# Real and imaginary PSUM tiles apart in a frequency-domain convolution with an MLP behind it, with taps between matmul groups and roots moved to GpSimd

## The chip, the cores and the metric

The kernel runs on one core of one Trainium2 chip. The metric is the device time of one execution in microseconds (us). The kernel before takes 347.24 us (median of the runs beside the changed kernel; 347.0 in the three runs that came first). A run that is more than 1.5% above the fastest of its kernel is labelled slow and left out of the ratios. Engines are called PE (TensorE matmul), PEld (its weight loads), DVE (VectorE), ACT (ScalarE) and POOL (GpSimd).

## The reference, cut to what matters

```python
S, D, ks, Dff = 2048, 512, 4, 1376                 # bfloat16 inputs, batch 1
kv = short_causal_conv(k, shift_k) * v             # 4 taps along the sequence
y  = irfft(rfft(kv padded to 2S) * rfft(ssm_k padded to 2S))[:S] + kv * ssm_D
h  = q + layernorm(q) * y
out = h + relu(layernorm(h) @ w1) @ w2
```

The kernel computes the long convolution as a two-stage DFT by matmul for `ssm_k` and for `kv`, a complex product, and a two-stage inverse DFT.

## The kernel before

These are the parts that the change touches. This program counts PSUM, the memory that matmuls write to, in banks of 512 fp32 values for each partition, and its largest pools hold eight of them. `u` and `psy` below are two banks each, with two buffers, which fills all eight.

```python
# product stage, 16 rounds kp
def product(kp):
    u = psum.tile([P, 2, 2, 256], F32, tag="u")            # real half s=0, imaginary half s=1
    usb = prod.tile([P, 2, 256 - NJ, 2], F32, tag="usb", bufs=2)
    for s in range(2):
        stage2(u[:, s, :, :], a1x, kp, s)                   # 4 matmuls of 256 columns, PE
        uj = u[:, s, :, :].rearrange("p k j -> p j k")
        nc.scalar.copy(out=usb[:, s, :, :], in_=uj[:, po, :])     # ACT, for GpSimd
        # ... t[s] = u * kf: columns dv on DVE from PSUM, columns po on GpSimd from usb

def finish():                                              # two rounds later
    psy = psum.tile([P, 2, 512], F32, tag="psy")
    for s, (a, b, m) in enumerate(...):
        # two matmuls of 512 columns into psy[:, s, :]
        nc.scalar.copy(out=kf[:, s, :, 2*kp:2*kp+2], in_=psy[:, s, :]...)   # ACT
# ...
# stage 1 of a DFT: 8 groups of 64 small matmuls (32 rows, 64 columns), 4 evacuations each
# taps: 16 blocks of 4 matmuls of 512 columns and one DVE multiply, after stage 2 of k
# ...
def inv2(q):                                               # pz is ONE tile of four banks
    for l4 in range(4):
        # 64 matmuls (32x32 by 128 columns) into pz[..., l4, :]
        nc.scalar.copy(out=zt[:, 4*q + l4, :]..., in_=pz[:, :, l4, :]...)   # ACT

def rstd(mv, r, q):                                        # row norms' roots
    nc.scalar.activation(out=r[:, ts, :], in_=mv[:, ts, 1:2], func=ACT.Sqrt, ...)
    nc.vector.reciprocal(out=r[:, ts, :], in_=r[:, ts, :])
# MLP: PSUM tiles of one bank, three buffers; transposes of the norm one token tile at a time, one buffer
```

## Time and profile before

The profiled run has a span of 344.8 us. The stages, read from the timeline, each from its first matmul to the first of the next (inverse stage 2 up to its own last matmul, and the entry from there):

| stage | before, us | granted PE clock |
|---|---|---|
| up to the first product | 87.2 | 0.5 to 1.0 by stage |
| products, 16 rounds | 100.1 | 0.50 |
| inverse stage 1 | 18.3 | 0.89 |
| inverse stage 2 | 35.2 | 0.54 |
| entry to the MLP | 6.65 | |
| MLP | 97.3 | 0.97 |

The first line of the page's busy part says why the average misleads; each entry is an engine, its busy time, its share of the span, and its instructions:

```profile
PE 254.9 (74%) x3094; PEld 169.8 (49%) x3104; DVE 163.0 (47%) x313; ACT 135.0 (39%) x240; POOL 54.3 (16%) x75
```

PE is the busiest with 74%, but 67 of its busy 255 us lie in a product stage that runs at half clock, where the same matmuls take up to twice as long. A busy share doesn't say whether an engine is the bound or is only slow; the clock row, the waits and the rounds do.

### The profile page before, as it was taken

How to read it: one execution, taken by the hardware profiler on the slowest of the kernel's cores; microseconds unless marked ns; L12 is line 12 of the kernel's file. 1: busy time of each engine (PE TensorE's matmuls, PEld its weight loads, DVE VectorE, ACT ScalarE, POOL GpSimd, SP SyncE). 2: the span in 40 equal slices, each digit the busy share in tenths (PEclk: the TensorE clock that was granted, in tenths of full speed). 3: DMA queues.
4: the chain of work that ended last, by engine and by line, in shares of the span. 5: the costliest groups of instructions: out<-in, count | busy, mean ns of one | idle time of the engine just before them, and what ended most of it. 6: DMA issues, size and time to landing. Idle time of an engine off the chain costs nothing.

```text
span 344.8 us, 7155 instructions
## 1 busy us (share of the span) xinstructions
PE 254.9 (74%) x3094; PEld 169.8 (49%) x3104; DVE 163.0 (47%) x313; ACT 135.0 (39%) x240; POOL 54.3 (16%) x75
## 2 busy tenths in 40 slices
PE   0765999966566666667667986666597887897994
PEld 0754994555544444445444983444243443343441
DVE  8966577677443223332331984400753483582111
ACT  3964560256123322233224892222353073162420
POOL 4694000000343223332333000000000000000000
PEclk9955899985555555555555995555589999999999
DMA  8990008000000000000002980000001101101101
GB/s 254 205 163 4 3 0 127 0 3 6 2 0 0 1 0 0 0 0 2 0 0 59 199 316 4 4 4 4 0 0 28 34 0 33 30 0 32 31 15 46
DMA packets 23663, 13.88 MB, mean 40 GB/s; under 512 B 19056, under 2 KB 22480, under 8 KB 23504
## 3 DMA queue, kind: packets, MB, share of 16 engines
q1 hardware_dynamic: 22560, 13.36, 16.3%
q8 instruction: 24, 0.39, 0.5%
q10 hardware_dynamic: 1072, 0.07, 0.3%
q14 instruction: 7, 0.06, 0.1%
HBM read 7.08 MB, written 2.10 MB: 27 GB/s over the span
## 4 chain that ended last, share of the span: by engine, by line
PE 66%; ACT 10%; DVE 10%; issue 3%; ACTq 0%; DVEq 0%
PE ps2m L495 11%; PE ps1m L482 10%; PE psy L332 10%; PE pz L420 7%; PE u L232 6%; PE psi L393 5%; DVE t L322 5%; PE pkv L282 4%; PE u L234 4%; ACT kf L334 3%; ACT zt L423 3%; PE ps2k L232 3%; PE ps2k L234 2%; ACT hlnT L470 2%; DVE st L433 2%
## 5 line engine op out<-in xcount | busy, mean ns | idle before, releaser
L322 DVE TENSOR_TENSOR t<-u,kf 128x704 fp32r<-128x704 f32 x32 | 28.5, 892 | 64.2 <-ACT usb L318 64.1
L482 PE MATMUL ps1m<-hlnT,w 128*128 128x512 bf16 (+1 forms) x175 | 41.3, 396 | 4.3 <-ACT h1T L484 3.3
L495 PE MATMUL ps2m<-w,h1T 128*128 128x512 bf16 (+1 forms) x169 | 38.8, 379 | 0.4
L322 POOL TENSOR_TENSOR t<-usb,kf 128x320 fp32r<-128x320 f32 x32 | 28.3, 886 | 65.0 <-ACT usb L318 64.9
L332 PE MATMUL psy<-t,ipos 128*128 128x512 f32 x48 | 29.2, 684 | 10.9 <-ACT kf L334 10.9
L420 PE MATMUL pz<-bp,ecore 32*32 32x128 f32 x1024 | 24.3, 406 | 11.8 <-ACT zt L423 10.9
L484 ACT ACTIVATE h1T<-ps1m 128x512 bf16<-128x512 f32 (+1 forms) x44 | 25.8, 595 | 18.0 <-PE ps1m L482 17.7
L232 PE MATMUL u<-a1x,c2n 128*128 128x256 f32 x32 | 16.0, 499 | 21.7 <-DVE t L322 21.7
L482 PEld LDWEIGHTS <-w 128*128 128x128 bf16 (+1 forms) x176 | 18.2, 104 | 26.9 <-issue 8.4
L498 DVE TENSOR_TENSOR o<-ps2m,xh 128x512 bf16<-128x512 f32 x16 | 11.1, 692 | 41.6 <-PE ps2m L495 41.6
L334 ACT CAST kf<-psy 128x512 fp32r<-128x512 f32 x32 | 19.2, 601 | 29.3 <-PE psy L332 29.3
L495 PEld LDWEIGHTS <-h1T 128*128 128x128 bf16 (+1 forms) x176 | 17.0, 98 | 20.0
L318 ACT COPY usb<-u 128x160 f32<-128x160 f32 x32 | 9.3, 292 | 42.8 <-PE u L234 42.8
L420 PEld LDWEIGHTS pz<-bp,ecore 32*32 32x32 f32 x1024 | 15.0, 134 | 20.8 <-ACT zt L423 17.6
L332 PEld LDWEIGHTS psy<-t,ipos 128*128 128x128 f32 x48 | 13.3, 318 | 22.7 <-ACT kf L334 22.5
L232 PEld LDWEIGHTS u<-a1x,c2n 128*128 128x128 f32 x32 | 10.0, 311 | 26.4 <-DVE t L322 26.4
L433 DVE BATCH_NORM_STATS2 st<-xh 128x6 f32<-128x512 bf16 x32 | 19.7, 678 | 0.0
L423 ACT CAST zt<-pz 128x512 bf16<-128x512 f32 x16 | 9.4, 584 | 24.2 <-PE pz L420 24.2
L393 PE MATMUL psi<-dre,kf 128*128 128x256 f32 x64 | 17.1, 304 | 0.7 <-ACT kf L334 0.7
L429 DVE RECIPROCAL rstd<-rstd 128x4 f32<-128x4 f32 x8 | 1.4, 178 | 34.0 <-ACT rstd L428 34.0
L470 ACT COPY hlnT<-pt 128x512 bf16<-128x512 bf16 x16 | 9.4, 585 | 20.2 <-PE pt L469 20.2
L393 PE MATMUL psi<-dim,kf 128*128 128x256 f32 x64 | 16.9, 301 | 0.0
(106 smaller groups left out, 479.2 us busy)
## 6 DMA issues: line engine op xcount, KB each, us to landing
sk<-in_A_ssm_k_dram SPq DMA_DIRECT2D x1, 2048.0 KB, 8.6
xh<-in_A_q_dram SPq DMA_DIRECT2D x4, 512.0 KB, 8.2
out_dram<-o SPq DMA_DIRECT2D x64, 32.0 KB, 1.6
w<-in_B_w_dram SPq DMA_DIRECT2D x1, 1376.0 KB, 15.2
w<-in_B_w_dram SPq DMA_DIRECT2D x1, 1280.0 KB, 17.8
w<-in_B_w_dram SPq DMA_DIRECT2D x1, 96.0 KB, 17.4
dtab<-in_A_ssm_D_dram ACTq DMA_DIRECT2D x2, 32.0 KB, 8.6
vT<-in_A_v_dram SPq DMA_TRANSPOSE x4, 5.3
```

The lines of the kernel that those rows point to most:

```text
L232: nc.tensor.matmul(out=ps[:, kk, :], lhsT=w_re[:, k1, :], rhs=a_in[:, k1, :], start=True, stop=False, skip_group_check=True)
L234: nc.tensor.matmul(out=ps[:, kk, :], lhsT=w_im[:, k1, :], rhs=a_in[:, 32 + k1, :], start=False, stop=True, skip_group_check=True)
L322: eng.tensor_tensor(out=t[:, :, j, :], in0=in0.unsqueeze(1).to_broadcast([P, 2, n, 2]), in1=kfr[:, :, j, ks], op=ALU.mult)
L332: nc.tensor.matmul(out=psy[:, s, :], lhsT=m_[:], rhs=t_.rearrange("p j k -> p (j k)"), start=first, stop=not first)
L334: nc.scalar.copy(out=kf[:, s, :, 2 * kp:2 * kp + 2], in_=psy[:, s, :].rearrange("p (j k) -> p j k", k=2))
L393: nc.tensor.matmul(out=ps[:, i, :], lhsT=kf[:, c, 4 * m:4 * m + 4, :].rearrange("p r k -> p (r k)"), rhs=d[:].rearrange("p a b -> p (a b)" ...
L420: nc.tensor.matmul(out=pz[32 * a:32 * a + 32, r4, l4, :], lhsT=ecore[rows, rho, n2, :], rhs=rhs, start=(rho == 0), stop=(rho == 1), tile_p ...
L423: nc.scalar.copy(out=zt[:, 4 * q + l4, :].rearrange("p (m r) -> p m r", r=4), in_=pz[:, :, l4, :].rearrange("p r m -> p m r"))
L433: nc.vector.bn_stats(out=st[:, i, :], in_=xh[:, 4 * q + i, :])
L482: nc.tensor.matmul(out=ps1[:fsz, :], lhsT=w1[:, c, fc * P:fc * P + fsz], rhs=hlnT[:, c, sc * SCW:(sc + 1) * SCW], start=(c == 0), stop=(c ...
L484: nc.scalar.activation(out=h1T[:fsz, fc, :], in_=ps1[:fsz, :], func=ACT.Relu)
L495: nc.tensor.matmul(out=ps2[:], lhsT=h1T[:ksz, fc, i * P:(i + 1) * P], rhs=w2[:ksz, fc, :], start=(fc == 0), stop=(fc == NFC - 1))
```

## The change

Its intent is to let every hand-over of a PSUM bank be double buffered by itself: the real and imaginary halves of `u` and `psy` become tiles of their own, and `pz` gets a second buffer. The taps, which use PE and DVE, go between the groups of stage 1 of k, which leaves both idle at times. The roots leave ACT's queue, where they stood ahead of the MLP's Relus. The MLP gets six PSUM buffers instead of three, and two token tiles share one transpose tile with two buffers. All loads of k and v are issued at the start. The taps and the transposes of kv now come ahead of stage 2 of k, and some copies move between ACT and DVE. Cut to its core:

```diff
-        u = psum.tile([P, 2, 2, 256], F32, tag="u", name="u")
-        usb = prod.tile([P, 2, 256 - NJ, 2], F32, tag="usb", name="usb", bufs=2)
         for s in range(2):
-            stage2(u[:, s, :, :], a1x, kp, s)
+            u = psum.tile([P, 2, 256], F32, tag=f"u{s}", name=f"u{s}")
+            stage2(u, a1x, kp, s)
+            usb = prod.tile([P, 256 - NJ, 2], F32, tag=f"usb{s}", name=f"usb{s}", bufs=2)
 ...
-        psy = psum.tile([P, 2, 512], F32, tag="psy", name="psy")
         for s, (a, b, m) in enumerate(...):
+            psy = psum.tile([P, 512], F32, tag=f"psy{s}", name=f"psy{s}")
 ...
-    stage1(kfl, a1k, "ADADADAD")
+    stage1(kfl, a1k, "ADAADADA", two_taps)      # two tap blocks after each of 8 groups
 ...                                             # the bulk tap loop after stage 2 of k goes
+    table(cc, r2)                               # second sine table: now just ahead of stage 1 of k
 ...
-    psum = pl.push("psM", bufs=3, space=PSUM)
+    psum = pl.push("psZ", bufs=2, space=PSUM)   # inverse stage 2 alone
-    pz = psum.tile([P, 4, 4, P], F32, name="pz", bufs=1)
     def inv2(q):
+        pz = psum.tile([P, 4, 4, P], F32, tag="pz", name="pz")
 ...
-        nc.scalar.activation(out=r[:, ts, :], in_=mv[:, ts, 1:2], func=ACT.Sqrt, bias=eps_t[:], scale=1.0)
-        nc.vector.reciprocal(out=r[:, ts, :], in_=r[:, ts, :])
+        nc.gpsimd.tensor_single_scalar(out=r[:, ts, :], in_=mv[:, ts, 1:2], scalar=EPS, op=ALU.add)
+        nc.gpsimd.tensor_tensor(out=r[:, ts, :], in0=r[:, ts, :], in1=mhalf[:, 0:4].unsqueeze(2), op=ALU.pow)
 ...
+    ptp = pl.push("psT", bufs=2, space=PSUM)    # transposes, two token tiles at a time
+    psum = pl.push("psM", bufs=6, space=PSUM)   # MLP
```

## The prediction

> **What bounds the kernel now.** I read the page's 40 slices first, to cut the span into stages, then the busy table over one stage, then the timeline inside each stage, because the limits differ from stage to stage.
>
> ```profile
> PE   0765999966566666667667986666597887897994
> PEclk9955899985555555555555995555589999999999
> ```
>
> One digit is 8.6 us. The long run of 5s in the clock row, slices 10 to 22, is the product stage (16 rounds `kp` of u, product, psy). The other low runs are stage 1 of k, stage 1 of x, and inverse stage 2 (slices 24 to 28). From the timeline the stages are: first transposes and stage 1 of k to 33.3 us, stage 2 of k to 51.0, taps to 65.7, transposes of kv to 73, stage 1 of x to 87.2, products to 187.3, inverse stage 1 to 204.4, inverse stage 2 to 240.8, MLP to 344.8. The product stage is 100.1 us, 29% of the span. Its busy times (columns PE, PEld, DVE, ACT, POOL, clock):
>
> ```profile
> 87.00:187.30 100.30, 66.79 (x192) 46.99 (x192) 28.54 (x33) 28.57 (x64) 28.71 (x36) 0.50 0.00 0
> ```
>
> No engine is full: PE 67%, the other three under 29%, and PE has half its clock throughout. So the stage is a chain of waits. The groups name them:
>
> ```profile
> L332 PE MATMUL psy<-t,ipos 128*128 128x512 f32 x48 | 29.2, 684 | 10.9 <-ACT kf L334 10.9
> ...
> L232 PE MATMUL u<-a1x,c2n 128*128 128x256 f32 x32 | 16.0, 499 | 21.7 <-DVE t L322 21.7
> ```
>
> PE waits 21.7 us for DVE and 10.9 us for ACT, 2.04 us in each of 16 rounds. The timeline of one round shows why:
>
> ```profile
> 138.69 0.29 ACT L318 COPY usb<-u 128x160 f32<-128x160 f32 x1 [0.30 <-PE u L234]
> 139.02 0.89 DVE L322 TENSOR_TENSOR t<-u,kf 128x704 fp32r<-128x704 f32 x1 [2.71 <-ACT usb L318]
> ...
> 139.96 0.58 PE L232 MATMUL u<-a1x,c2n 128*128 128x256 f32 x1 [1.36 <-DVE t L322]
> ...
> 142.08 0.60 ACT L334 CAST kf<-psy 128x512 fp32r<-128x512 f32 x1 [0.56 <-PE psy L332]
> ...
> 142.73 1.22 PE L332 MATMUL psy<-t,ipos 128*128 128x512 f32 x2 [0.69 <-ACT kf L334]
> ...
> 146.16 0.58 PE L232 MATMUL u<-a1x,c2n 128*128 128x256 f32 x1 [1.36 <-DVE t L322]
> ```
>
> The matmuls of the imaginary half of u (c2n) read nothing that DVE makes. They wait only because DVE still reads the real half of the same tile. psy is the same with ACT. The round is 146.16 - 139.96 = 6.20 us.
>
> Inverse stage 2 alternates PE and ACT in the same way, 2.20 us per token group, again at half clock. In the MLP, transposes go in steps with one PSUM buffer, and a Sqrt that waits for DVE blocks ACT's Relus behind it:
>
> ```profile
> 210.00 0.59 ACT L423 CAST zt<-pz 128x512 bf16<-128x512 f32 x1 [1.61 <-PE pz L420]
> 210.64 1.52 PE L420 MATMUL pz<-bp,ecore 32*32 32x128 f32 x64 [0.68 <-ACT zt L423]
> ...
> 265.37 0.39 PE L469 MATMUL pt<-ident,hln 128*128 128x128 bf16 x4 [0.67 <-ACT hlnT L470]
> ...
> 276.04 0.30 ACT L428 ACTIVATE rstd<-mv,eps_t 128x4 f32<-128x4 f32 x1 [7.55 <-DVE mv L435]
> ...
> 276.88 7.07 PE L482 MATMUL ps1m<-hlnT,w 128*128 128x512 bf16 x32 [1.66 <-ACT h1T L484]
> ```
>
> **What the Trainium skill says.** "PSUM — Partial Sum Buffer", section "PSUM bank collisions raise a hardware error", asks for guards by bank (or bank and quadrant), not wider. Each half of u and of psy is a whole bank (512 fp32), so the waits above are wider than needed and may go; ACT before DVE on one bank must stay. "TensorE: Matmul & The Clock Gate", Part 1, says that half clock is the default and that about 3.4 us of busy PE release full clock. The trace agrees: stage 2 of k runs without gaps from 33.8 us and its matmuls go from 0.213 to 0.12 us apart at 37.7; inverse stage 1 changes at 191.2 after a start at 187.3. "Runtime: NRT & Kernel Launch", section "Instruction fetch mechanics", says that instructions come in blocks of 256 and that crossing into the next is mostly hidden. In stage 1 it is not hidden here: after every 128 matmuls with 128 weight loads PE stops for 0.9 to 2.1 us on "issue". "ScalarE: Activation LUTs", section "Table sets", gives about 2.7 us for a table load; here it took 1.28.
>
> **The change, part by part.**
>
> *Product stage.* Work per round stays. PE at half clock: 8 x 0.213 + 4 x 0.427 (512 columns at the same 1.2 columns per ns; the timeline has 0.42, 140.99 to 141.41) = 3.41 us. At full clock: 8 x 0.12 + 4 x 0.216 (the MLP's spacing for 512 columns) = 1.82. DVE 2 x 0.892 = 1.78; ACT 2 x 0.292 + 2 x 0.601 = 1.79; POOL 2 x 0.886 = 1.77. With u0, u1, psy0, psy1 at two banks each (all 8 banks, as before) every hand-over is two rounds long. The longest loop is u, usb, t, u again: about 0.65 + 0.3 + 0.9, with up to 1.5 of queueing, against 2 x 1.85 = 3.7. So at half clock PE alone is the bound and is dense; dense work has released the clock above within 3 to 6 us; then four engines stand within 0.05 us of each other. I take 2.0 us per round for that balance. Stage: about 5 us cold for two rounds, 14 x 2.0 = 28, and 4 to 5 us of emptying = 38. Gain 62 us.
>
> *Before the products.* Taps were 14.7 us in which PE worked and ACT idled; stage 1 of k was 15.2 us in which PE stalled on "issue" and on evacuation. After: per group PE 0.52 (64 matmuls at full clock) + 8 x 0.216 = 2.25 us; DVE 1.5 evacuations x 0.684 + 2 taps x 0.692 = 2.41; ACT 1.5. DVE bounds it: 8 x 2.41 = 19.3. Instructions now arrive at 144 per 2.4 us, slower than the roughly 256 per 3.5 us that stage 1 reached, so the fetch gaps should hide. New cost: the second sine table (4.18 us on ACT) now stands before ACT's first evacuation, so little moves before 22 us. Stage 1 with taps ends near 40.5 us. Then transposes 6, stage 2 of k 16 x 0.96 = 15.4, stage 1 of x 14 as now (same fetch limit; its share moves a little to ACT): 40.5 + 6 + 15.4 + 14 = 76 us, taken as 77. The order before takes 87.2. Gain 10. The two extra transposing loads land by about 28 us (eight at 2.5 us behind the first at 9.3) and each chunk is wanted later than that.
>
> *Inverse stage 1* begins warm, but ACT is full there (20 copies x 0.593 + 8 sines x 0.72 = 17.6 us): gain 0.6.
>
> *Inverse stage 2.* `pz` is one tile per quarter, and four groups of a quarter share its banks; the changed program still waits for ACT inside a quarter. Only 3 of 15 hand-overs go: 3 x 0.66 = 2.0. The table load and the first Sqrt stood ahead of the first evacuation: 0.7. Gain 2.7.
>
> *Entry to the MLP.* 240.81 to 247.46 held Sqrt, reciprocal, norm and four transpose steps. After, the norm is ready earlier, 16 transposes take about 2.3 us and the last copy 1.0: 3.3. Gain 3.3.
>
> *MLP.* Three hooks of transposes: 3.39 us (264.31 to 267.70) become about 1.05; gain 7. Two Relu blocks of 1.66 us go; gain 3.3. The GpSimd add and power on 128x4 have no duration in this trace; small POOL rows take 0.1 to 0.4 us, and I allow 1 us for the pair (an estimate). DVE's path to the next norm is then 11.2 + 2 = 13.2 us against 14.3 us of PE work (66 matmuls x 0.216), so it stays off the path.
>
> Sum: 62 + 10 + 0.6 + 2.7 + 3.3 + 10.3 = 89. 347.0 - 89 = 258; I say 259.
>
> **Rivals.** (1) *The clock stays at half in the products.* For: PE was at 0.50 for 100 us with 67% busy, and stage 1 of x lost its full clock at about 75 us with PE near 60% busy. Against: both had gaps on PE; dense fp32 stages warmed each time. Then the stage is 16 x 3.41 + 4 = 58 and the time about 279. (2) *ACT becomes the bound*, as its FIFO mixes usb and kf: a late kf holds the next usb, which holds DVE and POOL. 2.4 us per round, time about 265. (3) *GpSimd's power is slow*, 3 us or more for a pair: then the norms come late in the MLP, two hooks wait some 3 us each, about 265. (4) *The front gains nothing*, since the sine table and DVE's taps eat it: 268.
>
> **Range and chances.** The product stage carries 70% of the gain and its clock is the largest doubt; I give rival 1 about 15%, which nearly sets the upper end at 280. The lower end, 247, needs 1.85 us per round and a front of 72 us. Even with rivals 1 and 4 together (about 288) it is faster by 17%. Faster 0.97, same 0.02, slower 0.01.
>
> **What would show it.** Products right: round near 2.0 us, clock near 1.0 after its first rounds, no PE wait on DVE for c2n while t's first half runs. Wrong: rounds of 3.4 us with PE full at 0.50. Front right: taps among stage 1's groups, few "issue" gaps, DVE near full from 22 to 40 us, first u matmul near 77 us. Inverse stage 2 right: still about 33 us, with PE waits on zt at 12 places. MLP right: no PE wait on hlnT between transposes and none on Relu after Sqrt. The prediction fails if waits by tile stay in the products, or if GpSimd's power shows microseconds that DVE and then PE wait for.

## The result, and the profile after

The changed kernel is correct and takes 248.88 us (median of 4 runs, 248.22 to 249.79), beside 347.24 us. The ratio is 0.717, with a 95% interval of 0.7142 to 0.7198. A ratio is the mean time of one kernel's fast runs over that of the other's in the same rounds, so it is not quite the ratio of the medians. Where a difference in us is given below for an experiment, it is (its ratio - 0.717) x 347.2.

The slices of the page after, to be read like those of before (one digit is now 6.2 us):

```profile
PE   0586998999667999989967767779999999999992
PEclk9999999999855999999975555569999999999999
```

The long run of 5s of the products is gone. What is left at half clock is the end of stage 1 of x with the first two product rounds (slices 11 and 12, counted from 0) and inverse stage 2 (slices 20 to 25). The page's busy line:

```profile
PE 209.8 (85%) x3088; PEld 144.6 (59%) x3104; DVE 152.9 (62%) x296; ACT 133.8 (54%) x232; POOL 65.3 (26%) x92
```

PE lost 45 us of busy time with the same matmuls, 35 of them in the products, by the clock. The busy times of the product stage (stretch, length, then PE, PEld, DVE, ACT, POOL, clock, DMA share, GB/s):

```profile
75.25:108.25 33.00, 32.13 (x192) 28.94 (x192) 27.02 (x33) 26.30 (x64) 29.12 (x37) 0.94 0.01 1
```

The stage fell from 100.1 to 33.0 us, and now all four engines are between 80% and 97% busy. The groups of this stage (line, engine, operation, tile, form, count, then busy us and mean ns, then the idle time ahead of them and its releaser):

```profile
L326 PE MATMUL psy<-t,ipos 128*128 128x512 f32 x48 | 15.8, 390 | 0.0
...
L316 DVE TENSOR_TENSOR t<-u,kf 128x704 fp32r<-128x704 f32 x32 | 27.0, 888 | 4.6 <-ACT usb L312 4.6
L316 POOL TENSOR_TENSOR t<-usb,kf 128x320 fp32r<-128x320 f32 x32 | 28.6, 927 | 3.2 <-ACT usb L312 2.4
```

PE's wait for the cast of `psy` went from 10.9 us to 0, and the group of `u` that waited 21.7 us for DVE no longer has an entry for it. DVE's products take what they took before (888 ns each, 892 before), but the idle time ahead of them is down to 4.6 us from 64.2. One round in the timeline of the changed kernel (start, length, engine, line):

```profile
96.85 0.39 PE L326 MATMUL psy<-t,ipos 128*128 128x512 f32 x1
97.01 1.69 DVE L316 TENSOR_TENSOR t<-u,kf 128x704 fp32r<-128x704 f32 x2 [0.19 <-ACT usb L312]
...
97.50 1.17 ACT L328 CAST kf<-psy 128x512 fp32r<-128x512 f32 x2
...
98.73 0.39 PE L326 MATMUL psy<-t,ipos 128*128 128x512 f32 x1
```

A round is 98.73 - 96.85 = 1.88 us, against 6.20. PE has no bracket, so it waits for nothing; DVE's two products of a round run back to back.

By stages, the gain of 344.8 - 246.4 = 98.4 us in the profiled spans is this:

| stage | before | after | gain | predicted gain |
|---|---|---|---|---|
| up to the first product | 87.2 | 75.25 | 11.9 | 10 |
| products | 100.1 | 33.0 | 67.1 | 62 |
| inverse stage 1 | 18.3 | 16.95 | 1.4 | 0.6 |
| inverse stage 2 | 35.2 | 32.3 | 2.9 | 2.7 |
| entry to the MLP | 6.65 | 3.85 | 2.8 | 3.3 |
| MLP | 97.3 | 85.1 | 12.2 | 10.3 |

This trace has the shortest front: in the traces of the eight experiments below that have the same front it took 76.0 to 77.0 us, so its gain is nearer to 10 or 11 us.

### The profile page after: what moved, and what is told of

Read it like the earlier page. It is cut to its first block, busy times and chain, and to the rows that moved or that the text cites. A ratio compares the mean times of both kernels' runs of the same rounds, so it can differ in the third digit from the quotient of the medians.

```text
span 246.4 us, 7166 instructions
## 1 busy us (share of the span) xinstructions
PE 209.8 (85%) x3088; PEld 144.6 (59%) x3104; DVE 152.9 (62%) x296; ACT 133.8 (54%) x232; POOL 65.3 (26%) x92
## 4 chain that ended last, share of the span: by engine, by line
PE 79%; ACT 10%; DMA 3%; DVE 3%; issue 2%; ACTq 0%
PE ps1m L479 16%; PE ps2m L492 15%; PE pz L416 10%; PE psi L389 6%; PE pst L196 5%; PE psy L326 5%; PE pkv L254 4%; PE u L226 4%; PE u L228 3%; DMA sk<-in_A_ssm_k_dram 3%; PE ps L212 3%; PE ps2k L228 3%; ACT zt L419 3%; PE ps2k L226 3%; ACT c2c L174 2%
## 5 line engine op out<-in xcount | busy, mean ns | idle before, releaser
L495 DVE TENSOR_TENSOR o<-ps2m,xh 128x512 bf16<-128x512 f32 x16 | 10.9, 689 | 49.3 <-PE ps2m L492 49.3
L479 PE MATMUL ps1m<-hlnT,w 128*128 128x512 bf16 (+1 forms) x175 | 39.9, 388 | 1.5 <-ACT hlnT L467 1.3
L316 DVE TENSOR_TENSOR t<-u,kf 128x704 fp32r<-128x704 f32 x32 | 27.0, 888 | 4.6 <-ACT usb L312 4.6
L424 POOL TENSOR_SCALAR rstd<-mv 128x4 f32<-128x4 f32 x8 | 1.8, 230 | 94.1 <-DVE mv L431 94.1
L467 ACT COPY hlnT<-pt 128x1024 bf16<-128x1024 bf16 x8 | 7.7, 1015 | 15.0 <-PE pt L466 15.0
L326 PE MATMUL psy<-t,ipos 128*128 128x512 f32 x48 | 15.8, 390 | 0.0
L389 PE MATMUL psi<-dim,kf 128*128 128x256 f32 x64 | 15.5, 283 | 0.0
L254 PE MATMUL pkv<-kT,wdiag 128*128 128x512 bf16 x56 | 14.8, 381 | 0.4
L196 PE MATMUL pst<-ident,sk 128*128 128x128 bf16 x64 | 6.7, 298 | 9.1 <-DMA sk<-in_A_ssm_k_dram 9.1
L201 ACT CAST a1k<-ps 128x512 fp32r<-128x512 f32 x20 | 10.4, 593 | 7.0 <-PE ps L212 7.0
L284 ACT CAST kf<-ps2k 128x512 fp32r<-128x512 f32 x16 | 10.2, 640 | 5.5 <-PE ps2k L228 5.3
```

The lines of the kernel that those rows point to most:

```text
L196: nc.tensor.transpose(out=pst[:, i, :], in_=src[:, :, :, 8 * q + i], identity=ident[:])
L254: nc.tensor.matmul(out=ps[:], lhsT=wdiag[:, rg, j, :], rhs=kT[c][:, rg, 16 - j:CH + 16 - j], start=(j == 0), stop=(j == KS - 1))
L316: eng.tensor_tensor(out=t[:, :, j, :], in0=in0.unsqueeze(1).to_broadcast([P, 2, n, 2]), in1=kfr[:, :, j, ks], op=ALU.mult)
L326: nc.tensor.matmul(out=psy[:], lhsT=m_[:], rhs=t_.rearrange("p j k -> p (j k)"), start=first, stop=not first)
L389: nc.tensor.matmul(out=ps[:, i, :], lhsT=kf[:, c, 4 * m:4 * m + 4, :].rearrange("p r k -> p (r k)"), rhs=d[:].rearrange("p a b -> p (a b)" ...
L479: nc.tensor.matmul(out=ps1[:fsz, :], lhsT=w1[:, c, fc * P:fc * P + fsz], rhs=hlnT[:, c, sc * SCW:(sc + 1) * SCW], start=(c == 0), stop=(c ...
```

## The experiments

Twelve kernels ran; all but two, whose arithmetic is wrong on purpose, compute the same as before. (These two passed the comparison with the reference as well, so its tolerance covers what they drop.) They are told by question.

### Are the separate tiles the whole of the product stage's gain, and which of them?

Four kernels. The first puts both tiles back into the changed kernel:

```diff
-            u = psum.tile([P, 2, 256], F32, tag=f"u{s}", name=f"u{s}")     # in the loop over s
+        u = psum.tile([P, 2, 2, 256], F32, tag="u", name="u")              # ahead of it
-            psy = psum.tile([P, 512], F32, tag=f"psy{s}", name=f"psy{s}")
+        psy = psum.tile([P, 2, 512], F32, tag="psy", name="psy")
```

> The kernel after with u and psy each in one tile of two banks again, everything else kept. Theory: the separate tiles alone give the 67 us of the product stage, so the time goes back from 249 to about 316 us and a product round from 1.88 to about 6.2 us at half clock. Rival: the gain came in good part from the other changes keeping the clock up; then the time rises by clearly less, to 265 to 290 us.

Measured: 319.82 us, ratio 0.9226 (0.9179 to 0.9273), 71 us slower. The product stage is 100.2 us at clock 0.50, as before the change to 0.1 us. Its timeline shows the old waits and the old round:

```profile
123.32 0.58 PE L226 MATMUL u<-a1x,c2n 128*128 128x256 f32 x1 [1.36 <-DVE t L316]
...
126.08 1.22 PE L326 MATMUL psy<-t,ipos 128*128 128x512 f32 x2 [0.69 <-ACT kf L328]
...
129.52 0.58 PE L226 MATMUL u<-a1x,c2n 128*128 128x256 f32 x1 [1.36 <-DVE t L316]
```

129.52 - 123.32 = 6.20 us. The theory holds, and the rival (the rest of the change keeps the clock up) falls.

The second puts only the split into the kernel before, with nothing else of the change:

```diff
 # kernel before
-        u = psum.tile([P, 2, 2, 256], F32, tag="u", name="u")
+            u = psum.tile([P, 2, 256], F32, tag=f"u{s}", name=f"u{s}")
-        psy = psum.tile([P, 2, 512], F32, tag="psy", name="psy")
+            psy = psum.tile([P, 512], F32, tag=f"psy{s}", name=f"psy{s}")
```

> The kernel before with u and psy split into real and imaginary tiles and nothing else of the change. Theory: 347 - 67 = about 280 us, with a product round of about 1.9 us at full clock. Rival: the split needs the rest of the change to bring the clock up; then the stage stays at half clock, about 3.5 us a round, and the time is 300 us or more.

Measured: 278.75 us, ratio 0.8041 (0.7999 to 0.8083), 68 us faster than before. Its product stage takes 34.0 us, with rounds of 1.88 us. The split alone does it, from either side.

The third and fourth join only one of the two in the changed kernel (the edit is one half of the first one's).

> The kernel after with only psy joined again in one tile of two banks; u stays split. Theory: TensorE then waits about 0.85 us a round for the first half's cast. With the clock kept that is about 2.7 us a round and about 262 us in all; if these waits also lose the clock, about 4.1 us a round and about 286 us. Rival: psy was not the tile that mattered, and the time stays within 3 us of 249.

Measured: 265.49 us, ratio 0.7659 (0.7613 to 0.7705), 17 us slower than after. The product stage is 47.8 us at clock 0.96; a round is 2.84 us. The theory with the clock kept holds.

> The kernel after with only u (and its copy usb) joined again; psy stays split. Theory: TensorE waits about 1.4 us a round for the copy and the product. With the clock kept that is about 3.2 us a round and about 270 us in all; if these waits also lose the clock, about 4.8 us a round and about 296 us. Rival: u was not the tile that mattered, and the time stays within 3 us of 249.

Measured: 278.36 us, ratio 0.803 (0.7973 to 0.8087), 30 us slower. The stage is 61.4 us at clock 0.89; a steady round is 3.53 us, not 3.2. Of the two forms of the theory it is the one with the clock kept, with the wait too small by 0.3 us: from the last matmul of one half over the copy and DVE's product to the first of the next half PE is free for 1.54 us, and the matmul after a wait takes 0.1 us more than the others: 1.88 + 1.54 + 0.1 = 3.5.

The two single costs in the stage are 47.8 - 33.0 = 14.8 and 61.4 - 33.0 = 28.4 us, together 43. Both joined cost 67. The missing 24 us fit the clock: PE's own work of a round is 3.41 us at half clock (the prediction's sum) and 1.88 at full, and 16 x 1.53 = 24.5. Why one joined tile reaches the full clock and two never do is suggested by how the stage starts with only `u` joined. Up to 85 us PE has four or eight matmuls in a row, then a wait; then the first `psy` matmuls fill the run:

```profile
85.40 0.58 PE L226 MATMUL u<-a1x,c2n 128*128 128x256 f32 x1 [1.36 <-DVE t L316]
...
88.77 0.35 PE L228 MATMUL u<-a1x,c2s 128*128 128x256 f32 x1
90.48 0.38 PE L226 MATMUL u<-a1x,c2n 128*128 128x256 f32 x1 [1.36 <-DVE t L316]
90.70 0.28 PE L228 MATMUL u<-a1x,c2c 128*128 128x256 f32 x1
```

From 85.40 to 88.8 PE had no wait, the first such run of 3.4 us in the stage, and at its end the clock rose (a matmul of 256 columns went from 0.41 to 0.28 us). With both joined, a wait for `psy`'s cast cuts the same run in two, of some 2.1 us each, and the clock stays low for all 100 us. Other starts agree in kind: with `psy` joined the clock rose 3.4 us after the first matmul, in the changed kernel 3.9, with the split alone 6.1, all in runs without a wait. The clock records in the packed traces say why these differ. In every one of the 14 traces the stretches between two changes of the clock are whole multiples of 3.41 us, so time is cut into slots. In all twelve traces whose products reached full clock, it rose at the end of the first slot in which PE was busy throughout (99% or more; the slot before had at most 83%). That is what the products show and no general threshold: in inverse stage 2 and at the start of the MLP it also rose after slots that the records show as 80 to 87% busy. With both tiles joined PE's longest run without a wait in this stage is 2.08 us, and no slot can be full. Where the slots fall is chance: it moves the length of the product stage between 32.8 and 34.1 us in kernels that have the same one. Once high, the clock stays high although PE then waits 1.4 us in each 3.53 us.

### Is PE alone the bound of the new round?

```diff
             for m_, t_, first in ((ipos, a, True), (m, b, False)):
+                w = 512 if first else 64                       # wrong on purpose
-                nc.tensor.matmul(out=psy[:], lhsT=m_[:], rhs=t_.rearrange("p j k -> p (j k)"),
+                nc.tensor.matmul(out=psy[:, 0:w], lhsT=m_[:], rhs=t_.rearrange("p j k -> p (j k)")[:, 0:w],
```

> The kernel after with the second matmul of each psy pair cut to 64 of its 512 columns: about 0.4 us less TensorE work a product round, a result that is wrong on purpose. Theory: the four engines are nearly balanced (TensorE 1.88, GpSimd 1.85, VectorE 1.8, ScalarE 1.76 us a round), so only minus 1 to 1.5 us. Rival: TensorE alone bounds the round and the others have slack; then 16 times 0.4, minus 6 to 7 us.

Measured: 247.68 us, ratio 0.7138 (0.7099 to 0.7176), so 1.1 us faster, which the intervals don't separate from 0. The stage is more telling. The steady round fell to 1.63 us, by 0.25 and not by 0.4, and DVE now has no idle time at all:

```profile
94.05 6.16 POOL L316 TENSOR_TENSOR t<-usb,kf 128x320 fp32r<-128x320 f32 x7
94.22 5.79 DVE L316 TENSOR_TENSOR t<-u,kf 128x704 fp32r<-128x704 f32 x7
```

So PE is the first bound. What holds the round at 1.63 us this run doesn't show. PE still has no wait in it: twice a round, behind a short matmul, the next spacing is 0.08 us wider than elsewhere, and 1.88 - 0.40 + 2 x 0.08 = 1.64. DVE is full as well: consecutive products overlap, so they start 0.82 us apart although each lasts 0.89 us, and 2 x 0.82 = 1.64. POOL doesn't keep up at all: its products start 0.87 us apart, 1.74 a round, and its last one starts 1.3 us after DVE's. So the near balance of the theory holds, with POOL some 0.14 us below PE, and the 6 to 7 us of the rival did not come. That the total met the theory is luck in part: in this run the clock rose only 5.9 us after the first product matmul, about 2 us later than in the changed kernel, and the stage shrank by only 1.7 us.

### What do the taps between the groups give?

```diff
-    stage1(kfl, a1k, "ADAADADA", two_taps)
+    stage1(kfl, a1k, "ADAADADA")
+    for gb in range(8):
+        two_taps(gb)
```

> The kernel after with the 64 tap matmuls' blocks all behind stage 1 of k again, not two after each group of it; loads and order otherwise as after. Theory: between the groups, the taps keep TensorE and VectorE busy while stage 1 waits for its copies and for instructions, so taking them out costs 6 to 9 us (about 256 us). Rival: the front's gain came from the earlier loads and the order of the stages alone; then the time stays within 2 us of 249.

Measured: 259.83 us, ratio 0.7483 (0.7444 to 0.7522), 10.9 us slower, so the theory's direction holds and its size is too small. Stage 1 of k alone and the taps alone, in this kernel (columns as above):

```profile
16.90:33.79 16.89, 8.67 (x512) 7.25 (x513) 7.92 (x14) 12.51 (x20) 11.60 (x14) 0.62 1.06 149
33.79:49.91 16.12, 16.12 (x69) 6.69 (x64) 11.67 (x17) 1.75 (x4) 0.00 (x0) 0.87 0.01 2
```

and both together in the changed kernel:

```profile
16.90:39.97 23.07, 19.61 (x569) 10.33 (x577) 19.36 (x32) 14.56 (x23) 11.58 (x14) 1.00 0.73 105
```

33.0 us against 23.1 (0.8 of these a last wait for DVE). Part of it is overlap: PE is busy for only 8.7 of 16.9 us in the bare stage. Part of it is the clock, which my expectation left out: bare stage 1 runs at 0.62 and hands its low clock to the taps, which take 16.1 us, where the kernel before, with its taps behind the dense stage 2 of k, needed 14.0. Interleaved, the clock is 1.00 throughout in this trace; in four other traces with the same interleaving it fell for one slot of 3.41 us near 22 us.

### What do the roots on GpSimd and the six buffers give in the MLP?

```diff
 # the roots on ACT and DVE again
-        nc.gpsimd.tensor_single_scalar(...add...)
-        nc.gpsimd.tensor_tensor(...pow...)
+        nc.scalar.activation(out=r[:, ts, :], in_=mv[:, ts, 1:2], func=ACT.Sqrt, bias=eps_t[:], scale=1.0)
+        nc.vector.reciprocal(out=r[:, ts, :], in_=r[:, ts, :])
```

> The kernel after with the row norms' roots back on ScalarE (square root) and VectorE (reciprocal), the six MLP buffers kept. Theory A: taking the square root off ScalarE is what removed the stalls of the MLP's first matmuls, so plus 4 to 6 us. Theory B: with six buffers TensorE has three more tiles, about 2.6 us, to run on while ScalarE loads its table, so only plus 1 to 2 us, from the entry to the MLP, where nothing covers the load.

```diff
 # three MLP buffers again
-    psum = pl.push("psM", bufs=6, space=PSUM)
+    psum = pl.push("psM", bufs=3, space=PSUM)
```

> The kernel after with three MLP buffers instead of six, the roots kept on GpSimd. Theory A and theory B alike: within 1 us of 249, since ScalarE keeps up with 1.7 us of matmuls a tile when no table load stops it. Rival C: the six buffers carry the MLP's gain by themselves, by covering the layer norms' other work on ScalarE; then plus 3 us or more.

Both edits together:

> The kernel after with both undone: roots on ScalarE and VectorE, three MLP buffers. Theory A: the same plus 4 to 6 us as with the roots alone undone. Theory B (either remedy is enough within the MLP): plus 4 to 5 us here, clearly more than the sum of the two single runs (1 to 2 and about 0).

| kernel | time, us | ratio (95%) | against after | MLP in the trace |
|---|---|---|---|---|
| after | 248.88 | 0.717 (0.7142 to 0.7198) | 0 | 85.1 |
| roots on ACT | 251.5 | 0.7241 (0.7216 to 0.7267) | +2.5 | 85.3 |
| three buffers | 249.04 | 0.7169 (0.7143 to 0.7194) | 0.0 | 85.7 |
| both | 255.07 | 0.735 (0.733 to 0.7369) | +6.2 | 89.9 |

Theory B holds: either remedy is enough inside the MLP, and only without both do the stalls of before come back:

```profile
189.65 0.30 ACT L424 ACTIVATE rstd<-mv,eps_t 128x4 f32<-128x4 f32 x1 [6.66 <-DVE mv L431]
190.48 7.07 PE L479 MATMUL ps1m<-hlnT,w 128*128 128x512 bf16 x32 [1.66 <-ACT h1T L481]
...
212.20 7.07 PE L479 MATMUL ps1m<-hlnT,w 128*128 128x512 bf16 x32 [1.66 <-ACT h1T L481]
```

These are 3.3 of the 4.8 us. The cause is the order in ACT's queue, as the first line shows: ACT waits 6.66 us for DVE's `mv`, and the Relus stand behind. The expectations above put it down to a table load; that is wrong, since the traces with the roots on ACT have no table load in the MLP (one at the start, one ahead of inverse stage 2). Another 1.2 us lie in the first 44 matmuls of the MLP, where the clock rose 5.5 us after the first one, against 3.1 in the changed kernel: that is where the slots fell, not the edit. With the roots alone on ACT, 0.9 us of the 2.5 are the entry to the MLP, where the root and the norm wait for each other (1.54 us between inverse stage 2 and the transposes, against 0.68); the rest isn't placed: in the trace the front is 1.4 us and the product stage 1.0 us longer, which this change doesn't touch and which differ by as much between other runs. On GpSimd the roots take this path (changed kernel, in the MLP):

```profile
186.40 0.23 POOL L424 TENSOR_SCALAR rstd<-mv 128x4 f32<-128x4 f32 x1 [32.77 <-DVE mv L431]
186.71 1.04 POOL L425 TENSOR_TENSOR rstd<-rstd,mhalf 128x4 f32<-128x4 f32 x1
187.78 1.38 DVE L436 TENSOR_SCALAR qln<-xh,mv,rstd 128x512 bf16<-128x512 bf16 x4 [1.47 <-POOL rstd L425]
```

DVE waits 1.47 us for the pair, more than for ACT's root and its own reciprocal, but no PE work waits for that norm.

### What bounds stage 1 of x and inverse stage 2?

In stage 1 of x, the changed kernel's trace puts PE's pauses down to "issue", waits for nothing that the profile shows, and I took them for the arrival of instructions. In inverse stage 2 PE waits 8.3 us in twelve places for ACT's copy. The first test halves the matmuls of stage 1 of x:

```diff
-                for f, first in ((f1hi, True), (f1lo, False)):
+                for f, first in ((f1hi, True),):               # for x only; wrong on purpose
```

> The kernel after with only the high part of the DFT matrix in stage 1 of x: half of its matmuls, a result that is wrong on purpose. Theory: with half the instructions to fetch and issue, the pauses that the trace puts down to issue halve, and the stage falls from 14 to about 10.5 us (minus 3 to 4 us). Rival: the copies out of PSUM on ScalarE and VectorE bound the stage; then it stays at 14 us and the time within 1 us of 249.

Measured: 245.7 us, ratio 0.7072 (0.7041 to 0.7102), 3.4 us faster; the stage is 10.5 us. The waits of PE on issue are gone, and short waits on ACT take their place, with ACT busy for 10.4 of the 10.5 us:

```profile
69.19 0.72 PE L212 MATMUL ps<-f_hi,xfl 32*128 32x64 bf16 x32 [0.25 <-ACT a1x L201]
```

So evacuation is the next bound, 3.5 us below. That the bound above it is the count of instructions, and not the matmuls' own time, this run can't tell, since it halves both; the next one can.

```diff
     def inv2(q):
-        pz = psum.tile([P, 4, 4, P], F32, tag="pz", name="pz")
         for l4 in range(4):
+            pz = psum.tile([P, 4, 4 * P], F32, tag="pz", name="pz")   # one per group, two buffers
```

> The kernel after with one pz tile for each group of four token tiles' matmuls (64 matmuls) and two buffers of it, so that every hand-over to ScalarE's copy is covered, not only three of fifteen. Theory: the 12 waits of about 0.66 us that remain in inverse stage 2 go, so minus 8 us at half clock (16 groups of 1.42 us in place of 33 us in all). If TensorE, now without pauses, is granted the full clock, minus 15 to 20 us, with ScalarE's copy of 0.59 us the bound. Rival: the waits are not for the bank but for the data's order, and the time stays within 1 us of 249.

Measured: 245.84 us median of 6 runs, two of which are labelled slow (the profiled one among them); the ratio of the fast ones is 0.7047 (0.7003 to 0.7091), 4.3 us faster. That is half of the smaller theory, and no full-clock gain. (The six runs spread evenly from 243.6 to 248.1 us; with the two slow ones the gain would be some 3 us.) I read the trace of the next kernel instead, which has the same edit and a fast profile:

```diff
 # in addition: the second sine table behind stage 1 of k
-    table(cc, r2)                              # ahead of it
     stage1(kfl, a1k, "ADAADADA", two_taps)
+    table(cc, r2)
```

> The kernel after with a pz tile for each group as in the run above, and the sine table of the DFT matrices built behind stage 1 of k instead of ahead of it. Theory: TensorE's wait of 2.1 us behind that table at the start of stage 1 goes, so about 2 us below the run with the pz tiles alone. Rival: the table is needed by stage 2 of k, which then starts as much later as stage 1 ends earlier; then no difference between the two.

Measured: 242.73 us (5 fast runs), ratio 0.6992 (0.696 to 0.7025). It is 1.9 us below the run with the pz tiles alone by the means of the fast runs (243.0 against 244.9), as the theory had it, though the two 95% intervals touch, so the size is uncertain; the traces have stage 1 of k with the taps from the first matmul to the last 2.45 us shorter, and stage 2 of k didn't wait. This version beats both kernels: 6.2 us better than the change as given. Its inverse stage 2, PE alone:

```profile
129.42 2.71 PE L416 MATMUL pz<-bp,ecore 32*32 32x128 f32 x128 [0.36 <-issue]
133.15 2.81 PE L416 MATMUL pz<-bp,ecore 32*32 32x128 f32 x128 [1.01 <-issue]
137.15 2.83 PE L416 MATMUL pz<-bp,ecore 32*32 32x128 f32 x128 [1.19 <-issue]
140.88 2.70 PE L416 MATMUL pz<-bp,ecore 32*32 32x128 f32 x128 [0.90 <-issue]
144.61 2.71 PE L416 MATMUL pz<-bp,ecore 32*32 32x128 f32 x128 [1.03 <-issue]
148.34 2.71 PE L416 MATMUL pz<-bp,ecore 32*32 32x128 f32 x128 [1.02 <-issue]
```

No wait on ACT's copy is left. In its place PE stops after every 128 matmuls, which with their weight loads are 256 instructions, and starts again 3.73 us after the last start (once 4.00, and 3.45 before the last 46 matmuls). The clock was 0.88 in this stage and did not help: a block at half clock (133.15 and 137.15) is done after 2.81 and 2.83 us, the others after 2.7, and all then wait. The whole stage, 1024 matmuls or 8 such blocks, takes 28.5 us to its last matmul, and 8 x 3.73 = 29.8 (it begins within a block, and its first 210 matmuls run without a pause). In the changed kernel, stage 1 of x has about the same period:

```profile
64.78 0.21 PE L212 MATMUL ps<-f_lo,xfl 32*128 32x64 bf16 x4 [0.99 <-issue]
...
68.51 0.24 PE L212 MATMUL ps<-f_lo,xfl 32*128 32x64 bf16 x4 [1.32 <-issue]
```

68.51 - 64.78 = 3.73 us, and 3.45 to the next start, for matmuls of a quite different shape. A nearly fixed period for a fixed count of instructions, in two stages with different work, speaks for the supply of instructions as the bound. The transfers themselves can be seen too: the page lists them (queue, count, MB, share of 16 engines; changed kernel).

```profile
q8 instruction: 24, 0.39, 0.6%
```

These are 24 packets of 16 KB. The run with half of stage 1 of x has 22, and issues 256 matmuls and 256 weight loads less: one packet is 256 instructions of PE. The packed trace has the time of each. In inverse stage 2 of the last kernel they come one at a time, 3.3 to 4.3 us from start to start, and take 0.9 to 1.4 us. All seven restarts of PE come 1.2 to 1.5 us after a packet has landed, and so do the three in stage 1 of x of the changed kernel. So the supply of instructions is the bound in both. Why the next packet isn't sent for sooner (it starts 1.0 to 1.7 us after PE does) stays open.

## Why the prediction was right or wrong, point by point

The prediction said 259.0 us, 247 to 280, and faster with 0.97. The time is 248.88, inside the range and near its lower end, and faster.

- **Waits by tile in the products: right.** Joining the tiles brings the 6.20 us round back, splitting them alone in the kernel before removes it. Rival 1 (half clock stays) did not occur; it doesn't even with one of the two tiles joined, only with both.
- **"I take 2.0 us per round for that balance": mis-sized, as were the two other terms of the stage, by about 1.5 us each.** The round is 1.88. PE's own sum, 8 x 0.12 + 4 x 0.23 = 1.88, is the whole of it: nothing had to be added for balance, since two products follow each other in 1.64 us on DVE and 1.74 on POOL. The 14 rounds took 26.5 us instead of 28, the two cold rounds 3.6 instead of 5 (full clock came 3.9 us after the first matmul), and the emptying 3.0 instead of 4 to 5. Stage 33.0 instead of 38, so 67.1 instead of 62. Up to 1 us of this is the luck of where the slots fell.
- **Front: right in size, wrong in its bound.** "DVE bounds it: 8 x 2.41" put the end near 40.5 us; it came at 40.0. Seven groups remained behind the stop at 21.65 us, at 2.45 us each in the steady part. But PE is the bound, as one group shows:

```profile
28.98 0.21 PE L212 MATMUL ps<-f_hi,kfl 32*128 32x64 bf16 x4
...
29.59 1.90 PE L254 MATMUL pkv<-kT,wdiag 128*128 128x512 bf16 x7
31.43 0.21 PE L212 MATMUL ps<-f_hi,kfl 32*128 32x64 bf16 x4
```

  The small matmuls take 29.59 - 28.98 = 0.61 us and the taps 1.84 (eight; one record is missing). PE has no wait above 0.16 us, and DVE, which needs 2.26 us a group because its instructions overlap a little, waits 1.4 us in all for PE. A tap matmul took the 0.216 us that I gave it; what I left out is 0.1 us at the change from taps to small ones, and the small ones take 0.61 instead of 0.52. The sine table did stop PE, for 2.08 us at 21.65, as predicted, and moving it is worth about 2 us. No gap on issue above 0.2 us was left in this stage, as predicted.
- **Inverse stage 1: 1.4 instead of 0.6.** It begins at full clock, as said, where before the first 4.0 us were at half. ACT is not quite full: its waits for PE fell from 2.9 to 1.7 us, which is most of the gain.
- **Inverse stage 2: right.** Three hand-overs went, the stage gained 2.9 us where 2.7 were predicted, and stayed at 32 us. The prediction did not see what stands under the waits: instructions arriving at about 3.7 us a block.
- **Entry: right**, 2.8 against 3.3.
- **MLP: 12.2 instead of 10.3.** Each hook of transposes (the place in the MLP where those of the next four token tiles run) costs 0.90 us instead of 1.05. The first matmuls of the MLP run 1.1 us shorter, which is luck: the clock rose 3.1 us after the first of them, against 5.3 before, by where the slots fell. The two Relu stalls were sized right (2 x 1.66), but their removal was put down to the roots alone; six buffers with the roots on ACT remove them too. Rival 3 (a slow power) fell: add and power took 0.23 + 1.04 us.
- **The lower end: a wrong sum.** 1.85 us per round and a front of 72 us, put into the prediction's own terms, give 259 - 14 x 0.15 - 5 = 252 us, not 247. Neither went that far; the time came near the lower end because the cold start, the emptying and the MLP were shorter too.

The six gains sum to 98.4 us where the prediction had 89; more than half of the missing 9 us is the product stage.

## What to carry to other kernels

Give every PSUM bank that changes hands between engines a tile of its own: here two tiles of two banks cost 67 of 347 us, 43 as waits and, by the sum above, 24 as half clock, since PE's longest run without a pause was 2.08 us and the clock rose in the products only after a full slot of 3.41 us. When waits are taken away one by one, expect the last one to pay for the clock as well, and test them singly and together. In a stage of very small matmuls count instructions: here 256 of them took 3.45 to 4.00 us to arrive, and neither a second buffer nor the full clock went below that.

## What the Trainium skill lacked or had wrong

- "Runtime: NRT & Kernel Launch", section "Instruction fetch mechanics": it calls the crossing into the next block of 256 instructions mostly hidden. With matmuls of 32 rows it was not: PE stopped after every 128 matmuls with 128 weight loads for 0.36 to 1.19 us, with a period of 3.45 to 4.00 us, in inverse stage 2 of the last kernel, and for 0.86 to 1.32 us in stage 1 of x of the changed one. No page gives a rate.
- "TensorE: Matmul & The Clock Gate", section "HAM oscillation": its abstract rule, no idle gaps of PE above about 3.4 us, is not enough here. In stage 1 of x of the changed kernel the clock fell from 1.00 to 0.50 at 65.5 us, with no gap of PE above 1.0 us before it; yet with `u` joined it stayed full through gaps of 1.4 us in every 3.53. What separates the two is open. In all 14 traces the falls lie in or right behind stages of 32-row matmuls, in the first transposes of the kernel before and its split, or at the very end, and none in the products; whether the 32 rows are the reason isn't tested. The rise after 3.4 to 6.1 us of unbroken work in the products, each time at the end of a full slot of 3.41 us, agrees with Part 1 of that page and its free-running window.
- "ScalarE: Activation LUTs", section "Table sets", gives about 2.7 us for a table load, and the prediction sets 1.28 us from the trace against it. That is no error of the page: elsewhere it counts 1.28 us for the load alone and the rest for a drain behind it. Every load in the traces looked at took 1.28 us.
- No page has a duration for a power on GpSimd: 1.03 us on average for 128x4 fp32, and 0.23 us for the scalar add ahead of it.
